# Retention attention and a GELU layer: one pipeline over six token chunks in place of two stages

## The chip, the cores and the metric

The kernel runs on one core of a Trainium2 chip. The core has five engines with a row of instructions each: TensorE (PE; PEld is its weight load), VectorE (DVE), ScalarE (ACT), GpSimd (POOL) and SyncE (SP), which here only issues transfers. ACT and POOL issue transfers too. An engine works through its row in order and waits at the head of it. SBUF is the working memory with 128 partitions; TensorE writes to PSUM, eight banks of 128 x 512 f32. The metric is device time in microseconds (us).

## The reference

Inputs are q, k and v of 4 batches, 8 heads, 768 tokens and 64 values, and two matrices. First a retention recurrence runs for each batch and head, then a dense layer with GELU over all 3072 tokens:

```python
gamma = 1.0 - 2.0 ** (-5.0 - np.arange(H))          # H = 8
scale = 1.0 / np.sqrt(D)                              # D = 64
for t in range(S):                                    # S = 768
    state = gamma * state + outer(k[:, :, t], v[:, :, t])
    y[:, :, t] = scale * (q[:, :, t] @ state)
x = y.transpose(0, 2, 1, 3).reshape(B * S, H * D)     # 3072 x 512
h = x @ w_in                                          # 512 x 2048
g = 0.5 * h * (1.0 + tanh(c * (h + 0.044715 * h**3))) # c = sqrt(2/pi)
return g @ w_out                                      # 2048 x 512, f32
```

Both kernels turn the recurrence into chunks of 128 tokens. Within a chunk, scores k.q are masked by decays and multiplied with v; what lies before the chunk enters through a 64 x 64 state of each head, which is carried on by a product of k and v.

## The kernel before, in words

It has two stages. **Attention** loops over four pairs of heads (`hp`). For a pair, POOL loads q, k and v of all batches and all six chunks (`_load_hp`, L94, L98, L102), cast from f32 to f16 on the way; every source piece is a row of 64 f32, 256 bytes. ScalarE scales q by decays (`_prep_q`, L110), VectorE scales k (`_prep_k`, L120). For each chunk, TensorE transposes q and k (L148, L153), ScalarE copies the result out of PSUM (L159), TensorE forms scores (L170), VectorE masks them (L181), and TensorE forms y within the chunk (L192), y from the state (L203) and the new state (L214). ScalarE and VectorE write y into `xT` (L222, L224), VectorE carries the state on (L228, L237).

**MoE** begins when all four pairs are done, since its first product sums over all heads. The two weight matrices are loaded by POOL in one transfer each, behind the last q, k and v (L246, L250). The loop goes over eight blocks of 384 tokens with four waves each; a wave makes four tiles h of 128 x 384 (L297, four matmuls each). GELU is written as h times a sigmoid: ScalarE copies h out of PSUM (L305), POOL squares it (L308), VectorE makes the inner polynomial in two operations (L310, L315), ScalarE takes the sigmoid (L320), VectorE multiplies (L322). The second product of the block before (L264, sixteen matmuls of 512 columns for 128 tokens) is put between the waves; VectorE copies it out (L272), SP stores it (L273).

The tile framework sets the order on each engine by its own scheduling, from the order of the code and the buffers that come free. It also gives transfers of a kind eight completion counters ("lanes") in turn: a transfer waits until the one eight before it has landed.

## Time and profile before

| | |
|---|---|
| median of the runs | 323.15 us |
| fastest run | 320.19 us |
| profiled execution, first to last instruction (its span) | 322.5 us |
| VectorE busy | 252.3 us, 78% of the span |
| TensorE busy | 241.7 us, 75% |
| TensorE's mean granted clock | 0.910 |

The profiled execution's time outside of its span isn't listed; the median of the runs lies 0.65 us above the span. A clock of 1 is 2.4 GHz, of 0.5 is 1.2 GHz. Busy matmul time counts the length of each matmul from its first read to its modelled end, and these overlap, so the pace of a row of matmuls is read from their starts. In the groups, the figures behind the bar are the busy time, the mean of one, and how long the engine stood idle just before, with the instruction whose end released it.

### The profile page before, as it was taken

The page shows a single profiled execution, that of the slowest core. Times are in us where ns is not written, and L with a number is a line of the kernel's source. Part 1 is how long each engine was busy: PE and PEld are TensorE (multiplying, and loading weights), DVE is VectorE, ACT ScalarE, POOL GpSimd, SP SyncE. Part 2 cuts the span into 40 slices and gives each one's busy share as a digit, 9 for nine tenths or more (in the row PEclk, how much of TensorE's full clock was granted, in tenths as well). Part 3 has the DMA queues.
Part 4 walks back from the last instruction along what each step waited for, and adds up shares of the span by engine and source line. Part 5 has one row for each costly group of instructions (what it writes and reads, how often), then busy time and mean ns, then how long its engine had stood idle before and what let it go on. Part 6 is the DMA issues. An engine that isn't in the chain of part 4 may idle for free.

```text
span 322.5 us, 5240 instructions
## 1 busy us (share of the span) xinstructions
PE 241.7 (75%) x1792; PEld 138.3 (43%) x1792; DVE 252.3 (78%) x528; ACT 166.6 (52%) x338; POOL 178.1 (55%) x214
## 2 busy tenths in 40 slices
PE   0257485278586786669889789869959969959985
PEld 0134373266474543325445345435524535525432
...
GB/s 138 140 138 139 141 140 136 142 142 202 196 123 0 2 0 1 2 0 33 34 35 33 35 35 33 33 34 35 34 33 29 38 33 1 67 35 0 48 84 65
DMA packets 81514, 20.82 MB, mean 65 GB/s; under 512 B 75728, under 2 KB 77776, under 8 KB 81488
## 3 DMA queue, kind: packets, MB, share of 16 engines
...
## 4 chain that ended last, share of the span: by engine, by line
DVE 64%; PE 13%; POOL 10%; issue 6%; ACT 4%; DMA 1%; DVEq 0%; ACTq 0%; POOLq 0%
DVE ww L315 23%; DVE t L310 14%; DVE g_sb L322 12%; DVE a_sb L181 8%; POOL pp L308 5%; ACT sg L320 3%; DVE kd L120 3%; PE yc_ps L203 3%; PE qkT_ps L148 3%; PE qkT_ps L153 2%; DVE s_new L228 2%; PE o_ps L264 2%; POOL qd L94 2%; POOL kp L98 2%; PE a_ps L170 1%
## 5 line engine op out<-in xcount | busy, mean ns | idle before, releaser
L308 POOL TENSOR_TENSOR pp<-hs 128x384 f16<-128x384 f16 x128 | 107.2, 858 | 129.9 <-DVE g_sb L322 64.6
L297 PE MATMUL h_ps<-xT,w_in_sb 128*128 128x384 f16 x512 | 96.1, 339 | 25.8 <-ACT hs L305 25.7
L320 ACT ACTIVATE sg<-ww 128x384 f16<-128x384 f16 x124 | 64.9, 524 | 81.7 <-DVE ww L315 81.2
L264 PE MATMUL o_ps<-w_out_sb,g_sb 128*128 128x512 f16 x384 | 87.6, 380 | 4.2 <-DVE g_sb L322 2.7
L315 DVE TENSOR_TENSOR ww<-t,hs 128x384 f16<-128x384 f16 x128 | 77.1, 602 | 7.5
L297 PEld LDWEIGHTS <-w_in_sb 128*128 128x128 f16 x512 | 51.6, 101 | 69.0 <-issue 37.6
L310 DVE TENSOR_SCALAR t<-pp 128x384 f16<-128x384 f16 x128 | 51.8, 405 | 8.7 <-POOL pp L308 8.7
L264 PEld LDWEIGHTS <-g_sb 128*128 128x128 f16 x384 | 37.5, 98 | 48.7 <-DVE g_sb L322 3.8
L305 ACT CAST hs<-h_ps 128x384 f16<-128x384 f32 x128 | 54.9, 472 | 3.3 <-PE h_ps L297 3.3
L322 DVE TENSOR_TENSOR g_sb<-hs,sg 128x384 f16<-128x384 f16 x124 | 51.1, 418 | 5.6 <-ACT sg L320 4.9
L120 DVE TENSOR_SCALAR kd<-kp,dec_sb 128x384 f16<-128x384 f16 x32 | 24.0, 774 | 20.5 <-DMA kp<-in_k_dram 20.5
L181 DVE TENSOR_TENSOR a_sb<-a_ps,msk_sb 128x512 f16<-128x512 f32 x48 | 29.2, 681 | 9.6 <-PE a_ps L170 9.6
...
L148 PE MATMUL qkT_ps<-iden_sb,qd 128*128 128x128 f16 x96 | 19.4, 294 | 17.8 <-ACT qd L110 17.4
L203 PE MATMUL yc_ps<-qkT_sb,s_new 64*64 64x128 f16 x160 | 12.7, 310 | 25.2 <-DVE s_new L228 15.7
L110 ACT ACTIVATE qd<-qd,dec_sb 128x384 f16<-128x384 f16 x32 | 19.0, 627 | 22.2 <-DMA qd<-in_q_dram 22.2
L222 ACT CAST xT<-yi_ps 128x512 f16<-128x512 f32 x24 | 13.9, 589 | 27.9 <-PE yi_ps L192 27.9
L159 ACT COPY qkT_sb<-qkT_ps 128x1024 f16<-128x1024 f16 x24 | 22.4, 1038 | 4.8 <-PE qkT_ps L153 4.8
L148 PEld LDWEIGHTS <-qd 128*128 128x128 f16 x96 | 13.1, 138 | 18.9 <-ACT qd L110 18.1
L102 POOL DMA_DIRECT2D vr<-in_v_dram x16 | 21.0, 1315 | 0.0
L224 DVE TENSOR_TENSOR xT<-xT,yc_ps 128x512 f16<-128x512 f16 x20 | 13.7, 683 | 9.2 <-PE yc_ps L203 8.2
...
## 6 DMA issues: line engine op xcount, KB each, us to landing
out_dram<-o_sb SPq DMA_DIRECT2D x24, 256.0 KB, 2.0
qd<-in_q_dram POOLq DMA_DIRECT2D x32, 96.0 KB, 4.3
kp<-in_k_dram POOLq DMA_DIRECT2D x32, 96.0 KB, 4.2
...
w_in_sb<-in_moe_w_in_dram POOLq DMA_DIRECT2D x1, 2048.0 KB, 15.5
w_out_sb<-in_moe_w_out_dram POOLq DMA_DIRECT2D x1, 2048.0 KB, 25.1
...
```

The lines of the kernel that those rows point to most:

```text
L94: nc.gpsimd.dma_start(out=qd[b][hp][:, :, j, :], in_=q[b, 2 * hp + j].rearrange("(c p) d -> p c d", p=128),)
L98: nc.gpsimd.dma_start(out=kp[b][hp][:, :, j, :], in_=k[b, 2 * hp + j].rearrange("(c p) d -> p c d", p=128),)
L148: nc.tensor.transpose(out=qkT_ps[:, b * 128:(b + 1) * 128], in_=qd[b][hp][:, c], identity=iden_sb,)
L181: nc.vector.tensor_tensor(out=a_sb[c][j], in0=a_ps[j], in1=msk_sb[:, 2 * hp + j].unsqueeze(1).broadcast_to([128, B, 128]), op=ALU.mult,)
L264: nc.tensor.matmul(out=o_ps, lhsT=g_tiles[fc][:, mi * 128:(mi + 1) * 128], rhs=w_out_sb[:, fc], start=(fc == 0), stop=(fc == 15),)
L297: nc.tensor.matmul(out=h_ps, lhsT=w_in_sb[:, kc, fc * 128:(fc + 1) * 128], rhs=xT[kc][:, bb * S + loc: bb * S + loc + MB], start=(kc == 0) ...
L305: nc.scalar.copy(out=hs[fc], in_=h_ps)
L308: nc.gpsimd.tensor_tensor(out=pp, in0=hs[fc], in1=hs[fc], op=ALU.mult)
L310: nc.vector.tensor_scalar(out=t1, in0=pp, scalar1=float(GA), scalar2=1.0, op0=ALU.mult, op1=ALU.add,)
L315: nc.vector.tensor_tensor(out=ww[fc], in0=t1, in1=hs[fc], op=ALU.mult)
L320: nc.scalar.activation(out=sg, in_=pww[fc], func=AF.Sigmoid, scale=sig_s)
L322: nc.vector.tensor_tensor(out=g_all[pmb][fc], in0=phs[fc], in1=sg, op=ALU.mult)
```

## The change

The program is one pipeline over six chunks of 128 tokens (times four batches, 512 columns for the MoE). `load` brings q, k and v of one chunk and batch as f32, 256 KB each with 1024 pieces of 256 bytes, by the queues of SP and ACT for the first chunk and SP alone later. `prep` scales q and k and casts v to f16: for the first chunk on VectorE (q), POOL (k) and ScalarE (v), later all on POOL. Attention works on one chunk and batch at a time in three pieces: T (`att_T`: eight transposes, one VectorE copy), A (`att_A`: eight score matmuls, two masks on VectorE) and Y (`att_Y`: y from the state and from the scores into one bank, the new state, VectorE's copies, and a scaling of the state on POOL). The three pieces share three PSUM banks. `moe1` makes one h tile of 512 columns and one ScalarE operation with GELU from PSUM to SBUF; `moe2` makes half of an output tile, or a share of it in the first chunk. The scheduling is switched off (`manual_schedule`), so engines keep the order of the code: `zip_units` puts the pieces of the next chunk between the matmul units of this one, twelve pieces on the first 22 of 24 units. Chunk 0 and chunk 1 split h tiles in halves of 256 columns. The weights are loaded by POOL in eight parts each. The scale of the decays moves from the mask and k to q, the mask is made on the chip from a triangle, and the state of a pair is kept as a 128 x 128 block with zeros beside its two heads.

The lines added (the lines removed are those of the listing above from the constants to the end of the function):

```diff
+    ctx.enter_context(tc.manual_schedule())
+    const = ctx.enter_context(tc.tile_pool(name="const", bufs=1))
+    ld = ctx.enter_context(tc.tile_pool(name="ld", bufs=2 * B))
+    pre = ctx.enter_context(tc.tile_pool(name="pre", bufs=2 * B))
+    att = ctx.enter_context(tc.tile_pool(name="att", bufs=3))
+    xp = ctx.enter_context(tc.tile_pool(name="xp", bufs=2))
+    gp = ctx.enter_context(tc.tile_pool(name="gp", bufs=2))
+    op = ctx.enter_context(tc.tile_pool(name="op", bufs=4))
+    psum = ctx.enter_context(tc.tile_pool(name="psum", bufs=1, space=bass.MemoryType.PSUM))
...
+    def load(c, b, engs):
+        for i, (nm, src) in enumerate(srcs):
+            t = ld.tile([128, H, Dh], F32, tag=f"{nm}32", name=f"{nm}32")
+            engs[i % len(engs)].dma_start(
+                out=t, in_=src[b, :, c * C:(c + 1) * C, :].rearrange("h p d -> p h d")
+            )
+            raw[nm, c, b] = t
+    SY, AC = nc.sync, nc.scalar
+    load(0, 0, (AC, SY, AC))
+    nc.sync.dma_start(out=iden, in_=iden_h.ap())
+    load(0, 1, (SY, AC, SY))
+    load(0, 2, (AC, SY, AC))
+    load(0, 3, (SY, AC, SY))
+    warm = const.tile([128, 1], F16)
+    nc.scalar.activation(out=warm, in_=cst[:, 0:1], func=AF.Gelu_apprx_tanh, scale=1.0)
+    st = const.tile([128, NHP, B, 128], F16, name="st")
+    nc.gpsimd.memset(st, 0.0)
...
+    for j in range(2):
+        for hp in range(NHP):
+            nc.vector.tensor_scalar(
+                out=mask[:, j, hp],
+                in0=cst[:, OT:OT + 128],
+                scalar1=float(1.0 / g128[2 * hp + j]),
+                scalar2=None,
+                op0=ALU.mult,
+            )
...
+    def prep(c, b):
+        for nm, col in (("q", OQ), ("k", OK)):
+            t = pre.tile([128, H, Dh], F16, tag=f"{nm}16", name=f"{nm}16")
+            eng = nc.vector if (c == 0 and nm == "q") else nc.gpsimd
+            eng.tensor_tensor(
+                out=t,
+                in0=raw.pop((nm, c, b)),
+                in1=cst[:, col:col + H].unsqueeze(2).broadcast_to([128, H, Dh]),
+                op=ALU.mult,
+            )
+            h16[nm, c, b] = t
+        t = pre.tile([128, H, Dh], F16, tag="v16", name="v16")
+        if c == 0:
+            nc.scalar.copy(out=t, in_=raw.pop(("v", c, b)))
+        else:
+            nc.gpsimd.tensor_copy(out=t, in_=raw.pop(("v", c, b)))
+        h16["v", c, b] = t
...
+    def att_T(c, b):
+        ps = psum.tile([128, 2, NHP, 128], F16, tag="att", bufs=3, name="qkT_ps")
+        for i, nm in ((0, "q"), (1, "k")):
+            for hp in range(NHP):
+                nc.tensor.transpose(
+                    out=ps[:, i, hp], in_=pair(h16[nm, c, b], hp), identity=iden
+                )
+        t = att.tile([128, 2, NHP, 128], F16, tag="qkT", name="qkT")
+        nc.vector.tensor_copy(out=t, in_=ps)
+        qkT[c, b] = t
...
+    def att_A(c, b):
+        t = qkT[c, b]
+        ps = [
+            psum.tile([128, NHP, 128], F32, tag="att", bufs=3, name=f"a_ps{j}")
+            for j in range(2)
+        ]
+        for hp in range(NHP):
+            for j in range(2):
+                nc.tensor.matmul(
+                    out=ps[j][:, hp],
+                    lhsT=t[j * 64:(j + 1) * 64, 1, hp],
+                    rhs=t[j * 64:(j + 1) * 64, 0, hp],
+                    start=True,
+                    stop=True,
+                )
+        for j in range(2):
+            s = att.tile([128, NHP, 128], F16, tag=f"a{j}", name=f"a_sb{j}")
+            nc.vector.tensor_tensor(out=s, in0=ps[j], in1=mask[:, j], op=ALU.mult)
+            a_sb[c, b, j] = s
...
+    def att_Y(c, b):
+        vv = h16["v", c, b]
+        kk = h16["k", c, b]
+        y_ps = psum.tile([128, NHP, 128], F32, tag="att", bufs=3, name="y_ps")
+        if c > 0:
+            for hp in range(NHP):
+                nc.tensor.matmul(
+                    out=y_ps[:, hp],
+                    lhsT=st[:, hp, b],
+                    rhs=qkT[c, b][:, 0, hp],
+                    start=(hp == 0),
+                    stop=False,
+                    skip_group_check=True,
+                )
+        for hp in range(NHP):
+            for j in range(2):
+                nc.tensor.matmul(
+                    out=y_ps[j * 64:(j + 1) * 64, hp],
+                    lhsT=vv[:, 2 * hp + j],
+                    rhs=a_sb[c, b, j][:, hp],
+                    start=(c == 0),
+                    stop=True,
+                    skip_group_check=True,
+                )
+        if c + 1 < NCk:
+            s_ps = psum.tile([128, NHP, 128], F32, tag="att", bufs=3, name="s_ps")
+            for hp in range(NHP):
+                nc.tensor.matmul(
+                    out=s_ps[:, hp], lhsT=pair(kk, hp), rhs=pair(vv, hp), start=True, stop=True
+                )
+        if b == 0:
+            xT[c] = xp.tile([128, NHP, B * C], F16, tag="x", name="xT")
+        nc.vector.tensor_copy(out=xT[c][:, :, b * C:(b + 1) * C], in_=y_ps)
+        if c + 1 < NCk:
+            for j in range(2):
+                sl = slice(j * 64, (j + 1) * 64)
+                if c == 0:
+                    nc.vector.tensor_copy(out=st[sl, :, b, sl], in_=s_ps[sl, :, sl])
+                else:
+                    nc.vector.tensor_tensor(
+                        out=st[sl, :, b, sl],
+                        in0=s_ps[sl, :, sl],
+                        in1=stg[sl, :, b, sl],
+                        op=ALU.add,
+                    )
+            if c + 2 < NCk:
+                nc.gpsimd.tensor_tensor(
+                    out=stg[:, :, b],
+                    in0=st[:, :, b],
+                    in1=cst[:, OG:OG + NHP].unsqueeze(2).broadcast_to([128, NHP, 128]),
+                    op=ALU.mult,
+                )
...
+    NQ = 8
...
+    w_in_sb = [const.tile([128, NHP, FQ * 128], F16, name=f"w_in{i}") for i in range(NQ)]
+    w_out_sb = [const.tile([128, FQ, d_model], F16, name=f"w_out{i}") for i in range(NQ)]
...
+    def load_w_in(i):
+        nc.gpsimd.dma_start(
+            out=w_in_sb[i],
+            in_=moe_w_in.rearrange("(kc p) n -> p kc n", p=128)[
+                :, :, i * FQ * 128:(i + 1) * FQ * 128
+            ],
+        )
...
+    def moe1(c, fc, t0=0, t1=B * C):
+        h_ps = psum.tile([128, B * C], F32, tag="h", bufs=3, name="h_ps")
+        for kc in range(NHP):
+            nc.tensor.matmul(
+                out=h_ps[:, t0:t1],
+                lhsT=w_in_sb[fc // FQ][:, kc, (fc % FQ) * 128:(fc % FQ + 1) * 128],
+                rhs=xT[c][:, kc, t0:t1],
+                start=(kc == 0),
+                stop=(kc == NHP - 1),
+            )
+        if t0 == 0:
+            g_sb[c, fc] = gp.tile([128, B * C], F16, tag=f"g{fc}", name="g")
+        nc.scalar.activation(
+            out=g_sb[c, fc][:, t0:t1],
+            in_=h_ps[:, t0:t1],
+            func=AF.Gelu_apprx_tanh,
+            scale=1.0,
+        )
+    o_ps = {}
...
+    def moe2(c, b, fcs, tag="o", bufs=2):
+        if fcs[0] == 0:
+            o_ps[c, b] = psum.tile([128, d_model], F32, tag=tag, bufs=bufs, name="o_ps")
+        ps = o_ps[c, b]
+        for fc in fcs:
+            nc.tensor.matmul(
+                out=ps,
+                lhsT=g_sb[c, fc][:, b * C:(b + 1) * C],
+                rhs=w_out_sb[fc // FQ][:, fc % FQ],
+                start=(fc == 0),
+                stop=(fc == NF - 1),
+            )
+        if fcs[-1] == NF - 1:
+            o_sb = op.tile([128, d_model], F32, tag="o", name="o_sb")
+            if b == B - 1:
+                nc.vector.tensor_copy(out=o_sb, in_=ps)
+            else:
+                nc.scalar.copy(out=o_sb, in_=ps)
+            nc.sync.dma_start(out=out[b * S + c * C:b * S + (c + 1) * C, :], in_=o_sb)
...
+    def zip_units(units, pieces):
+        done = 0
+        for i, u in enumerate(units):
+            u()
+            want = min(len(pieces), ((i + 1) * len(pieces) + len(units) - 1) // len(units))
+            while done < want:
+                fn[pieces[done][0]](pieces[done][1], int(pieces[done][2]))
+                done += 1
+    for b in range(B):
+        prep(0, b)
+        if b == 2:
+            for i in range(NQ):
+                load_w_in(i)
+    for i in range(NQ):
+        load_w_out(i)
+    for b in range(B):
+        load(1, b, (SY,))
+    run(0, "T0 T1 A0 T2 A1 Y0 T3 A2 Y1 A3 Y2")
+    half = 2 * C
+    for fc in range(0, 2):
+        moe1(0, fc, 0, half)
+    run(0, "Y3")
+    for fc in range(2, 8):
+        moe1(0, fc, 0, half)
+    for fc in range(0, 8):
+        moe1(0, fc, half, 2 * half)
+    for fc in range(8, 16):
+        moe1(0, fc)
+    for b in range(B):
+        prep(1, b)
+    for b in range(B):
+        load(2, b, (SY,))
+    units = [
+        (lambda e=e: [
+            moe2(0, b, [2 * e, 2 * e + 1], *(("o", 2) if b < 2 else ("h", 3)))
+            for b in range(B)
+        ])
+        for e in range(8)
+    ]
+    zip_units(units, [(p[0], 1, p[1]) for p in "T0 T1 A0 A1 Y0 Y1".split()])
+    def std_pieces(c):
+        return [
+            (p[0], c, p[1]) for p in "T0 T1 A0 T2 A1 Y0 T3 A2 Y1 A3 Y2 Y3".split()
+        ]
+    for c in range(1, NCk):
+        if c + 2 < NCk:
+            for b in range(B):
+                load(c + 2, b, (SY,))
+        if c == 1:
+            units = [(lambda fc=fc: moe1(c, fc, 0, half)) for fc in range(NF)]
+            zip_units(units, [(p[0], 1, p[1]) for p in "T2 T3 A2 A3 Y2 Y3".split()])
+            units = [(lambda fc=fc: moe1(c, fc, half, 2 * half)) for fc in range(NF)]
+        else:
+            units = [(lambda fc=fc: moe1(c, fc)) for fc in range(NF)]
+        units += [
+            (lambda b=b, hf=hf: moe2(c, b, list(range(hf * 8, hf * 8 + 8))))
+            for b in range(B)
+            for hf in range(2)
+        ]
+        pieces = []
+        if c + 1 < NCk:
+            for b in range(B):
+                prep(c + 1, b)
+            pieces = std_pieces(c + 1)
+        if pieces:
+            zip_units(units[:-2], pieces)
+            for u in units[-2:]:
+                u()
+        else:
+            for u in units:
+                u()
```

ScalarE in the MoE. Before, in the middle of the stage (`hs` is the copy of h, `sg` the sigmoid):

```order
L320 ACTIVATE sg<-ww 128x384
L305 CAST hs<-h_ps 128x384 x2
L320 ACTIVATE sg<-ww 128x384 x4
L305 CAST hs<-h_ps 128x384 x3
L320 ACTIVATE sg<-ww 128x384
```

Now, from the last cast of v for the first chunk to the output copies of chunk 1 (`g` is the GELU's result):

```order
L119 CAST v_169<-v_107 128x512
L249 ACTIVATE g<-h_ps 128x256 x16
L249 ACTIVATE g<-h_ps 128x512 x8
L275 COPY o_sb<-o_ps 128x512 x3
L249 ACTIVATE g<-h_ps 128x256 x32
L275 COPY o_sb<-o_ps 128x512 x3
```

The copies and sigmoids that alternate on ScalarE have become one operation a tile; output copies stand between the chunks.

VectorE at the start of the program. Before (`kd` is the scaled k):

```order
L120 TENSOR_SCALAR kd_0_0_87<-kp_0_86,dec_sb 128x384 x2
L120 TENSOR_SCALAR kd_1_0_96<-kp_0_95,dec_sb 128x384 x2
L120 TENSOR_SCALAR kd_2_0_105<-kp_0_104,dec_sb 128x384 x2
L120 TENSOR_SCALAR kd_3_0_114<-kp_0_113,dec_sb 128x384 x2
L120 TENSOR_SCALAR kd_0_1_139<-kp_1_138,dec_sb 128x384
L181 TENSOR_TENSOR a_sb_257<-a_ps_247,msk_sb 128x512
L181 TENSOR_TENSOR a_sb_259<-a_ps_248,msk_sb 128x512
```

Now (`q` are the four scaled q of chunk 0, `qkT` the transposed q and k, `a_sb` masked scores, `st` the state):

```order
L96 TENSOR_SCALAR mask<-cst 128x128 x8
L110 TENSOR_TENSOR q_139<-q_84,cst 128x512
L110 TENSOR_TENSOR q_145<-q_91,cst 128x512
L110 TENSOR_TENSOR q_151<-q_97,cst 128x512
L110 TENSOR_TENSOR q_165<-q_103,cst 128x512
L139 COPY qkT<-qkT_ps 128x1024 x2
L159 TENSOR_TENSOR a_sb_235<-a_ps_225,mask 128x512
L159 TENSOR_TENSOR a_sb_237<-a_ps_226,mask 128x512
L139 COPY qkT<-qkT_ps 128x1024
L159 TENSOR_TENSOR a_sb_260<-a_ps_250,mask 128x512
L159 TENSOR_TENSOR a_sb_262<-a_ps_251,mask 128x512
L195 CAST xT<-y_ps 128x4x128
```

All four scalings of q stand ahead of the first copy of transposed q and k, which ScalarE made before.

POOL behind the loads of the weights. Before:

```order
L102 DMA vr_3_901<-in_v_dram 128x12x64
L246 DMA w_in_sb<-in_moe_w_in_dram 128x4x2048
L250 DMA w_out_sb<-in_moe_w_out_dram 128x16x512
L308 ISA
L308 TENSOR_TENSOR pp<-hs 128x384 x128
```

Now (`stg` is the state scaled for the next chunk, `q`, `k` and `v` are those of chunk 1):

```order
L230 DMA w_out_137<-in_moe_w_out_dram 128x2x512
L230 DMA w_out_138<-in_moe_w_out_dram 128x2x512
L209 TENSOR_TENSOR stg<-st,cst 128x4x128 x4
L110 TENSOR_TENSOR q_536<-q_179,cst 128x512
L110 TENSOR_TENSOR k_538<-k_181,cst 128x512
L121 CAST v_540<-v_183 128x512
L110 TENSOR_TENSOR q_542<-q_185,cst 128x512
```

The squares are gone; scalings of the state and then those of the next chunk's q and k stand behind the last weight transfer, and in each later chunk again four `stg` ahead of the next `q`.

## Rows read from the trace of the kernel before

**Rows 1.** The page, part 1: busy us, share of the span, instructions.
```profile
PE 241.7 (75%) x1792; PEld 138.3 (43%) x1792; DVE 252.3 (78%) x528; ACT 166.6 (52%) x338; POOL 178.1 (55%) x214
```

**Rows 2.** Windows of three stretches: length, busy us of each engine, granted clock, DMA.
```profile
core 0: us, PE busy (x) PEld busy (x) DVE busy (x) ACT busy (x) POOL busy (x), PEclk, DMA share, GB/s
20.00:111.50 91.50, 61.63 (x872) 46.94 (x872) 69.06 (x112) 49.06 (x73) 51.98 (x61) 0.76 1.51 127
111.50:309.50 198.00, 168.91 (x863) 85.69 (x861) 175.97 (x401) 110.57 (x255) 107.22 (x128) 0.97 0.07 27
309.50:322.50 13.00, 8.07 (x35) 3.34 (x35) 3.85 (x9) 0.98 (x2) 0.00 (x0) 1.00 0.21 81
```

**Rows 3.** The page, part 4: the chain of waits by line.
```profile
DVE ww L315 23%; DVE t L310 14%; DVE g_sb L322 12%; DVE a_sb L181 8%; POOL pp L308 5%; ACT sg L320 3%; DVE kd L120 3%; PE yc_ps L203 3%; PE qkT_ps L148 3%; PE qkT_ps L153 2%; DVE s_new L228 2%; PE o_ps L264 2%; POOL qd L94 2%; POOL kp L98 2
```

**Rows 4.** The page, part 5: groups of the MoE stage (columns: heading of part 5).
```profile
## 5 line engine op out<-in xcount | busy, mean ns | idle before, releaser
L297 PE MATMUL h_ps<-xT,w_in_sb 128*128 128x384 f16 x512 | 96.1, 339 | 25.8 <-ACT hs L305 25.7
...
L264 PE MATMUL o_ps<-w_out_sb,g_sb 128*128 128x512 f16 x384 | 87.6, 380 | 4.2 <-DVE g_sb L322 2.7
L315 DVE TENSOR_TENSOR ww<-t,hs 128x384 f16<-128x384 f16 x128 | 77.1, 602 | 7.5
...
L310 DVE TENSOR_SCALAR t<-pp 128x384 f16<-128x384 f16 x128 | 51.8, 405 | 8.7 <-POOL pp L308 8.7
L322 DVE TENSOR_TENSOR g_sb<-hs,sg 128x384 f16<-128x384 f16 x124 | 51.1, 418 | 5.6 <-ACT sg L320 4.9
```

**Rows 5.** Timeline of TensorE (start us, length us): attention, first slow, later fast.
```profile
20.46 0.29 PE L148 MATMUL qkT_ps<-iden_sb,qd 128*128 128x128 f16 x1 [3.52 <-ACT qd L110]
...
21.18 0.31 PE L153 MATMUL qkT_ps<-iden_sb,kp 128*128 128x128 f16 x1
...
46.89 0.22 PE L153 MATMUL qkT_ps<-iden_sb,kp 128*128 128x128 f16 x1
...
47.79 0.22 PE L153 MATMUL qkT_ps<-iden_sb,kp 128*128 128x128 f16 x1
47.94 0.62 PE L170 MATMUL a_ps<-qkT_sb 64*128 64x128 f16 x16
...
51.22 0.41 PE L192 MATMUL yi_ps<-a_sb,vr 128*64 128x128 f16 x7
```

**Rows 6.** DMA packets from 10 to 60 us, and issues (KB each, us to landing).
```profile
DMA packets 54666, 6.95 MB, mean 139 GB/s; under 512 B 54661, under 2 KB 54661, under 8 KB 54661
...
out_dram<-o_sb SPq DMA_DIRECT2D x24, 256.0 KB, 2.0
qd<-in_q_dram POOLq DMA_DIRECT2D x32, 96.0 KB, 4.3
...
w_out_sb<-in_moe_w_out_dram POOLq DMA_DIRECT2D x1, 2048.0 KB, 25.1
```

**Rows 7.** Single lines: operation, count: duration ns min/median/max, first and last start, shape.
```profile
L181 DVE TENSOR_TENSOR a_sb<-a_ps,msk_sb x48: 677/680/693, 24.6 to 102.3; 128x512 f16<-128x512 f32 x48
...
L222 ACT CAST xT<-yi_ps x24: 564/586/640, 29.0 to 110.5; 128x512 f16<-128x512 f32 x24
...
L237 DVE CAST s_new<-st_ps x4: 410/410/414, 32.4 to 102.9; 128x256 f16<-128x256 f32 x4
...
L159 ACT COPY qkT_sb<-qkT_ps x24: 1012/1034/1072, 20.9 to 96.4; 128x1024 f16<-128x1024 f16 x24
...
L272 DVE COPY o_sb<-o_ps x24: 677/684/692, 147.6 to 318.6; 128x512 f32<-128x512 f32 x24
...
L315 DVE TENSOR_TENSOR ww<-t,hs x128: 344/360/999, 114.8 to 309.8; 128x384 f16<-128x384 f16 x128
...
L308 POOL TENSOR_TENSOR pp<-hs x128: 820/827/1033, 113.6 to 308.3; 128x384 f16<-128x384 f16 x128
```

**Rows 8.** Timeline of the end, all engines (start us, length us).
```profile
311.24 7.30 PE L264 MATMUL o_ps<-w_out_sb,g_sb 128*128 128x512 f16 x33 [0.35 <-DVE g_sb L338]
311.81 7.82 SPq L273 DMA_DIRECT2D out_dram<-o_sb  x4
```

303 lines of the change are left out of this document (33 added, 270 removed).

## The prediction

> **What bounds the kernel now.** I read the page first, for busy times, then the stages by windows, then the chain of waits, then the groups of the long stage, and last the pace of single matmuls. VectorE is busiest at 252.3 us, TensorE has 241.7 [rows 1]. In the table by stage the reader is to see three stretches: up to 111.5 us attention runs while the loads come in, with TensorE at a mean clock of 0.76; from there to 309.5 us the MoE runs with VectorE busy 176.0 of 198.0 us; 13 us end it [rows 2]. The chain runs over VectorE lines L315, L310 and L322, the GELU written out [rows 3]. Their groups sum to 77.1 + 51.8 + 51.1 = 180 us [rows 4], the MoE stage itself. The same stage's matmuls need less: 33 of 512 columns take 7.30 us, so (7.30 - 0.38)/32 = 0.216 us each, at full clock [rows 8]; all MoE work is 768 such matmuls (512 of 384 columns are worth 384, and 384 of 512 [rows 4]), or **166 us**. So half of the span lies in two places: 111 us before the first MoE matmul, and 32 us of the stage in which TensorE waits for VectorE.
>
> **What goes.** The GELU chain (POOL square, three VectorE operations, a ScalarE copy and a sigmoid per tile) leaves; one ScalarE operation from PSUM stands for it. A ScalarE cast of 128x512 out of PSUM takes 0.586 us [rows 7]; no row shows GELU, but the sigmoid is one table function per tile too and is no multiple of a copy, so I take 0.59 (0.37 for half a tile). 72 whole and 48 half tiles are 60 us in all; each stands behind 4 matmuls of 0.216, so 0.59 runs under 0.86. I cost it at nothing; its cover is gone only above 0.86 us a tile. VectorE loses 180 us and keeps evacuations: per (chunk, batch) a qkT copy, two masked scores at 0.68, y at about 0.68, two state pieces at about 0.41 [rows 7], some 4.4 us, 24 times, or about 105 us of the run. VectorE bounds nothing after the opening. **TensorE does.**
>
> **TensorE's work.** MoE 166 us. Attention per (chunk, batch): 8 transposes and 8 full matmuls (4 from the state, 4 for it) of 128 columns at (47.79 - 46.89)/16 = 0.056 us; 8 score and 8 y matmuls that run in pairs, 0.62 us for 16 and 0.41 for 7, so about 0.03 each [rows 5]. That is 0.9 + 0.5 = 1.4 us; the first chunk has no state to read and the last none to write. 20 pairs after the first chunk give 27 us less 20 x 0.05 for the last chunk, 26 us. Remaining after the opening: 166 + 26 = **192 us**.
>
> **The opening.** Twelve loads of 1024 pieces of 256 bytes, spread over the queues of SP and ACT, replace the loads from POOL that cast. Before, 54661 such pieces passed in 50 us, 0.915 ns each, so 0.94 us for a load if the new queues are as quick; if they didn't overlap at all a load would cost the 4.3 us that one of 768 pieces takes to land; a store of 256 KB lands in 2.0 [rows 6]. I take 0.94, since its pieces are the same reads of 256 bytes, and keep the other end for the rivals. VectorE has all four q scalings in its row before the first qkT copy, so it waits for the fourth q, which is about the tenth load: 1 + 10 x 0.94 + 2 to land + 0.75 to scale = 13 us. From there VectorE's own row sets the time: 3 copies before y of batch 0, one after, 3 masked pairs, y and state of batch 0, y of batch 1. For a copy of 1024 f16 from PSUM no row of VectorE exists; 512 f32 take 0.684, so 1.22 us by element, and ScalarE took 1.034 for it [rows 7]. With 1.22: 4 x 1.22 + 3 x 1.36 + 1.5 + 0.7 = 11 us, then y's state pieces and the fourth pair's first half, which free the two score banks, 1.5 us, and about 1.5 for handing on at three banks, with transposes at the 0.103 us of the first ones [rows 5]. The first MoE matmul starts at **27 us** (20 to 37). The Trainium skill (VectorE: DVE Perf Modes, The perf-mode tier table) has a copy of 16-bit data from PSUM at up to twice the rate. By that the four copies would cost 2.2 us less and the sum 2 us less; no run here shows it.
>
> The weights come beside. Before, both were issued together and had landed after 25.1 us [rows 6], at most 1.6 us for each of the sixteen pieces. POOL issues the first at about 11 us, and the second chunk's loads (11 us of transfer) share the rings, so the last piece of w_in lands between 11 + 13 + 2 = 26 and 37 us; it is asked for at 27 + 12. No wait, or one of 1 us. POOL is held by its row: the last w_out issue waits for a lane that the last w_in frees, then four state scalings, then the second chunk's q and k. POOL's two-input operation takes 0.827 us for 384 elements [rows 7], so 1.1 for 512. From 37 us: 4.4 + 2.2 more is 44; TensorE asks at 27 + 14 + 1.7 = 43. I take 0 to 1 us here, inside the small waits below.
>
> **Stalls at the seams.** In POOL's row the scaling of a chunk stands behind the last state scaling of the chunk before it, and that behind VectorE's state pieces of the last batch. From the end of that piece on TensorE: 1.7 us VectorE, 1.1 state, 2.2 for q and k, so 5 to 6 us; each further batch 2.9 (a cast of v at about 0.6). In the chunks with whole tiles TensorE has 3 pieces of 1.73 and one of 0.86 us to do first, 6 us; the first batch doesn't wait, the second about 1 us. Three chunks, 3 us. In chunk 1 the units are half tiles of 0.43 us, and the last piece lies three units before: TensorE waits about 4, then 2, then 0.5 us, **6 us**, and in this stage idle stretches of 2 us have gone with a clock under 1 (0.97 on the mean [rows 2]); I add 2 us. Sixty pieces in chunks 1 to 5 wait a little for a bank or a copy; before, TensorE waited 4.2 us in all ahead of 384 o matmuls, always for VectorE [rows 4], so I put 0.08 us on each, 5 us (0 to 18).
>
> **The end** is as before: from the last matmul (311.24 + 7.30) to the end of the span 4 us, with copy and store [rows 8].
>
> **Sum:** 27 + 192 + 3 + 6 + 2 + 5 + 4 = 239 us of span, against 322.5. The median of the runs lies 0.65 us over that span, so **240 us**.
>
> **The rivals.**
> (a) *The forecast*, 228 to 254: TensorE bound from about 27 us, with seams of 1 to 6 us. 0.62.
> (b) *No seams.* If POOL's operations are shorter or VectorE copies in half the time, the opening ends near 22 and waits shrink to 4 us: 22 + 192 + 4 + 4 = 222, up to 228. For it: POOL's row above is for 384 f16 elements and VectorE's for f32. Against it: the order in POOL's row is fixed. 0.13.
> (c) *Slower loads.* Pieces of 256 bytes on the queues of SP and ACT have no row. At 2 us a load the fourth q comes 10 us later: 250. At 3 us, 20 later, and twelve loads take 36 us while a chunk has 33 us of TensorE work (27.6 MoE and 5.4 attention): 262. For it: the store's 2.0 and the landing of 4.3 us. Against it: those are times of one, and many are in flight. 0.14, over 250 to 290.
> (d) *VectorE's evacuations held by POOL.* L315 reads two SBUF operands and took 0.344 to 0.999 us, with POOL's square beside it; the copy out of PSUM, L272, stayed within 0.677 to 0.692 [rows 7]. The masked scores and state sums read PSUM and one SBUF operand, and no row shows one beside POOL arithmetic. If each is held half of the time for 0.6 us, forty pieces slip by 0.5 us: 260. The Trainium skill (GPSIMD Engine Reference, Key points) says that POOL shares its SBUF interfaces with VectorE and that two SBUF inputs collide; L315 agrees, and by that page these operations, with one, would not. 0.08.
> (e) *Slower than before: loads set the pace of all.* Seventy-two loads at x us, and after the last of them about 45 us (scaling, the last attention, its MoE of 28 us, the end): 72x + 45. It passes 323 at x = 3.9 us and 329 at 3.95, so it decides where loads hardly overlap, at the landing time of 4.3 us. Against it: before, pieces of the same size passed at 0.94 us per 1024 with several landing at once. 0.03.
>
> The likeliest time is 240. To hold 8 in 10 the range takes (a) whole, most of (b) and the nearer half of (c) and (d): **222 to 264**. A change under 2% can't be told from none here. Faster by more: (a) to (d), 0.96; the same: a strip of (e), 0.01; slower: 0.03.
>
> **What will show it.** First qkT copy on VectorE near 13 us and first h matmul near 27. Twelve loads landed by 16 us. GELU at about 0.59 us and under 0.86. In chunks 2 to 4 a period of 34 to 36 us, with TensorE idle before transposes, released by POOL's q or k. In chunk 1 three such waits, the first of about 4 us. The matmul pace of 0.216 unchanged. If TensorE's idle time lies before score or y matmuls, released by VectorE, (d) is right; if before transposes, with POOL waiting for loads, (c) or (e). The forecast is wrong if TensorE is idle for more than 25 us after the first h matmul.

## The result: 239.1 us, and the profile after

The changed kernel takes 239.13 us (median of 4 runs, 238.1 to 240.66), the kernel before 323.94 in the runs beside it: a ratio of 0.7413, 95% interval 0.735 to 0.7477. The ratio leaves out one of the four runs of the kernel before, a slow one of 477 us, which the median of 323.94 includes. The forecast was 240. The profiled execution took 239.32 us, with a span of 237.5 us and a mean granted clock of 0.986.

The page of the changed kernel, part 1 (busy us, share of the span, instructions), part 4 (the chain of waits) and part 5 (groups, columns as in [rows 4]):

```profile
PE 216.5 (91%) x1600; PEld 118.6 (50%) x1600; DVE 87.0 (37%) x154; ACT 75.5 (32%) x144; POOL 85.8 (36%) x101
...
PE 85%; POOL 5%; DMA 5%; DVE 2%; SPq 1%; issue 1%; POOLq 0%
...
L240 PE MATMUL h_ps<-xT,w_in 128*128 128x512 f16 (+1 forms) x480 | 93.8, 344 | 0.0
L263 PE MATMUL o_ps<-w_out,g 128*128 128x512 f16 x384 | 86.9, 379 | 0.0
L249 ACT ACTIVATE g<-h_ps 128x512 f16<-128x512 f32 (+1 forms) x120 | 61.4, 512 | 76.1 <-PE h_ps L240 74.7
```

Against [rows 1] VectorE falls from 252.3 to 87.0 us, and TensorE, busy for 75% of a longer span, is busy for 91% of this one. The chain, which ran over three VectorE lines [rows 3], is TensorE's own work for 85%. Ahead of the h and o matmuls it stood idle for 25.8 and 4.2 us [rows 4]; now 0.0 for both. ScalarE, with GELU, waits 74.7 us for h_ps, and no wait of TensorE ends on ScalarE.

The same kernel's windows (columns as in [rows 2]), cut at the first h matmul and around chunk 1's seam, and five microseconds inside that seam:

```profile
0.00:24.50 24.50, 10.76 (x100) 7.22 (x101) 13.95 (x30) 3.75 (x6) 14.37 (x20) 1.00 1.18 219
24.50:60.00 35.50, 35.50 (x270) 21.50 (x268) 11.43 (x22) 13.63 (x30) 20.09 (x23) 1.00 1.17 209
60.00:80.00 20.00, 16.73 (x169) 12.30 (x169) 9.51 (x16) 7.75 (x21) 12.28 (x14) 0.83 1.02 251
80.00:220.00 140.00, 140.00 (x1011) 71.68 (x1006) 51.44 (x87) 48.30 (x85) 39.07 (x45) 1.00 0.29 78
...
72.00:77.00 5.00, 4.51 (x32) 2.86 (x30) 1.38 (x2) 0.99 (x3) 5.00 (x7) 0.50 0.95 214
```

The 111.5 us ahead of the first MoE matmul [rows 2] are 24.5. From there TensorE is idle in one place only, between 60 and 80 us (3.3 us), and that is also the only one of the four windows with a granted clock under 1: 0.83 on the mean, and 0.50, the level of 1.2 GHz, from 72 to 77 us. The last 64 matmuls start at 219.54 us, so the end is 4 us behind them, as in [rows 8]:

```profile
219.54 13.98 PE L263 MATMUL o_ps<-w_out,g 128*128 128x512 f16 x64
```

TensorE's longest waits behind its start are one of 4.1 us for VectorE's first qkT copy, in the opening, and one of 2.2 us for a q that POOL scales. Its timeline at the second place (start us, length us; idle before and releaser in brackets):

```profile
70.86 0.45 PE L135 MATMUL qkT_ps<-iden,q 128*128 128x128 f16 x4 [2.22 <-POOL q L110]
71.86 0.61 PE L135 MATMUL qkT_ps<-iden,k 128*128 128x128 f16 x4 [0.56 <-POOL k L110]
...
74.42 0.61 PE L135 MATMUL qkT_ps<-iden,k 128*128 128x128 f16 x4 [0.39 <-POOL k L110]
74.82 1.91 PE L240 MATMUL h_ps<-xT,w_in 128*128 128x256 f16 x8
...
78.41 0.39 PE L135 MATMUL qkT_ps<-iden,q 128*128 128x128 f16 x4
...
78.86 1.04 PE L240 MATMUL h_ps<-xT,w_in 128*128 128x256 f16 x8
```

The seam of chunk 1 (the place where chunk 2's first pieces wait for POOL) has three waits for POOL's scalings, 2.22, 0.56 and 0.39 us. After the first of them four transposes take 0.61 us and eight matmuls of 256 columns 1.91; at 78.4 the same take 0.39 and 1.04. So the seam costs twice: the idle time, and about as much again in slow matmuls.

Where the forecast's terms went (forecast, then measured, us):

| term | forecast | after |
|---|---|---|
| first h matmul | 27 | 24.55 |
| MoE, 768 matmuls of 0.216 | 166 | 166: 64 in 13.98, or 0.216 each |
| attention of 20 pairs | 26 (1.4 each, less 1 in all) | 34.7 (1.78 each, less 0.9) |
| seams of chunks 2 to 4 | 3 | 0 |
| seam of chunk 1, idle and clock | 6 + 2 | 3.3 + 3.1 |
| small waits | 5 | about 0 |
| end | 4 | 4.0 |
| not assigned by the forecast | | 1.9 |
| span | 239 | 237.5 |

Of the 1.9 us, 0.7 are chunk 0's last piece (26.39 to 27.10 us) and 1.0 are the first eight matmuls of 256 columns at the slow pace (1.84 us from start to the next start, for 0.87 at 0.109 each); 0.2 is unassigned. The 3.1 is counted from the timeline: from 70.86 to 78.41 us lie 0.95 us of idle time and matmuls that take 3.5 at the full pace. An experiment below gives the same.

### The profile page after: what moved, and what is told of

Read it like the earlier page. It is cut to its first block, busy times and chain, and to the rows that moved or that the text cites. A ratio compares the mean times of both kernels' runs of the same rounds, so it can differ in the third digit from the quotient of the medians.

```text
span 237.5 us, 3948 instructions
## 1 busy us (share of the span) xinstructions
PE 216.5 (91%) x1600; PEld 118.6 (50%) x1600; DVE 87.0 (37%) x154; ACT 75.5 (32%) x144; POOL 85.8 (36%) x101
## 4 chain that ended last, share of the span: by engine, by line
PE 85%; POOL 5%; DMA 5%; DVE 2%; SPq 1%; issue 1%; POOLq 0%
PE h_ps L240 35%; PE o_ps L263 35%; PE qkT_ps L135 4%; PE y_ps L179 3%; DMA k<-in_k_dram 3%; PE a_ps L150 3%; POOL w_in L222 3%; PE s_ps L190 2%; PE y_ps L169 2%; POOL k L110 2%; DMA v<-in_v_dram 2%; SPq L72 1%; DVE a_sb L159 1%; POOL q L110 0%; DVE st L202 0%
## 5 line engine op out<-in xcount | busy, mean ns | idle before, releaser
L240 PE MATMUL h_ps<-xT,w_in 128*128 128x512 f16 (+1 forms) x480 | 93.8, 344 | 0.0
L263 PE MATMUL o_ps<-w_out,g 128*128 128x512 f16 x384 | 86.9, 379 | 0.0
L249 ACT ACTIVATE g<-h_ps 128x512 f16<-128x512 f32 (+1 forms) x120 | 61.4, 512 | 76.1 <-PE h_ps L240 74.7
L240 PEld LDWEIGHTS <-w_in 128*128 128x128 f16 x480 | 45.7, 100 | 32.0 <-issue 0.2
L263 PEld LDWEIGHTS <-g 128*128 128x128 f16 x384 | 36.5, 98 | 41.6
L159 DVE TENSOR_TENSOR a_sb<-a_ps,mask 128x512 f16<-128x512 f32 x48 | 30.9, 686 | 24.6 <-PE a_ps L150 24.3
L209 POOL TENSOR_TENSOR stg<-st,cst 128x512 f32<-128x512 f16 x16 | 16.5, 1040 | 49.3 <-DVE st L202 48.0
L195 DVE CAST xT<-y_ps 128x512 f16<-128x512 f32 x24 | 16.6, 691 | 35.0 <-PE y_ps L179 35.0
L110 POOL TENSOR_TENSOR k<-k,cst 128x512 f16<-128x512 f32 x24 | 25.1, 1046 | 7.0 <-DMA k<-in_k_dram 7.0
L110 POOL TENSOR_TENSOR q<-q,cst 128x512 f16<-128x512 f32 x20 | 20.9, 1043 | 2.8 <-DMA q<-in_q_dram 2.8
```

The lines of the kernel that those rows point to most:

```text
L110: eng.tensor_tensor(out=t, in0=raw.pop((nm, c, b)), in1=cst[:, col:col + H].unsqueeze(2).broadcast_to([128, H, Dh]), op=ALU.mult,)
L159: nc.vector.tensor_tensor(out=s, in0=ps[j], in1=mask[:, j], op=ALU.mult)
L195: nc.vector.tensor_copy(out=xT[c][:, :, b * C:(b + 1) * C], in_=y_ps)
L209: nc.gpsimd.tensor_tensor(out=stg[:, :, b], in0=st[:, :, b], in1=cst[:, OG:OG + NHP].unsqueeze(2).broadcast_to([128, NHP, 128]), op=ALU.mult,)
L240: nc.tensor.matmul(out=h_ps[:, t0:t1], lhsT=w_in_sb[fc // FQ][:, kc, (fc % FQ) * 128:(fc % FQ + 1) * 128], rhs=xT[c][:, kc, t0:t1], start= ...
L249: nc.scalar.activation(out=g_sb[c, fc][:, t0:t1], in_=h_ps[:, t0:t1], func=AF.Gelu_apprx_tanh, scale=1.0,)
```

## The experiments

The theory: TensorE sets the end; the gain is VectorE's 180 us taken off GELU, which lets attention lie between MoE matmuls under the loads; what is left to win is the seam of chunk 1 and the opening. The rivals that were tried: one half of the change does it all; the loads set the pace; the opening is bound by something other than its order.

**The changed kernel again**, as the base of the runs on the same chip.

> The changed kernel as it is, timed on the same chip as the three variants sent with it: 237 to 241 us, ratio 0.735 to 0.748.

239.19 us, ratio 0.7447 [0.7409, 0.7485], span 236.9. The opening differs a little between executions: here the first h matmul starts at 23.73 us and the first o matmul at 39.43, in the execution above at 24.55 and 40.12.

**GELU alone**: the kernel before, with one ScalarE operation for the six.

```diff
-            nc.scalar.copy(out=hs[fc], in_=h_ps)
...
-            nc.vector.tensor_tensor(out=ww[fc], in0=t1, in1=hs[fc], op=ALU.mult)
+            nc.scalar.activation(out=g_all[mb][fc], in_=h_ps,
+                                 func=AF.Gelu_apprx_tanh, scale=1.0)
```

> The kernel before with GELU as one ScalarE operation and nothing else changed. If the MoE stage then runs at TensorE's pace: 111.5 us before it, 166 to 174 in it, 5 at the end, so 283 to 291 us, ratio 0.88 to 0.90. If GELU made most of the gain: 260 or less. If it made nothing of it: 315 or more.

285.26 us, ratio 0.8819 [0.8746, 0.8893]. The window of its MoE stage:

```profile
111.50:270.00 158.50, 158.50 (x854) 83.98 (x853) 15.21 (x22) 62.72 (x128) 0.00 (x0) 0.99 0.09 34
```

TensorE is never idle in it; the stage ahead, with 61.6 us of 91.5 busy, is that of [rows 2]. 38 us of the 84 are GELU's, and 46 are left to the rest of the change.

**The pipeline with GELU written out** as before (ScalarE copy and POOL square at once; `gelu2`, two VectorE operations, two tiles later; `gelu3`, the sigmoid and VectorE's product, another two later; ahead of the second half of each output tile, and of every unit of `moe2` in chunk 0, all pending tiles are finished at once).

```diff
-        nc.scalar.activation(
-            out=g_sb[c, fc][:, t0:t1],
...
+        nc.scalar.copy(out=hs[:, :n], in_=h_ps[:, t0:t1])
+        nc.gpsimd.tensor_tensor(out=pp[:, :n], in0=hs[:, :n], in1=hs[:, :n], op=ALU.mult)
+        stage.append([g_sb[c, fc][:, t0:t1], hs, pp, None, n])
+        if len(stage) >= 3:
+            gelu2(stage[-3])
+            if len(stage) >= 5:
+                gelu3(stage.pop(0))
```

> The pipeline and its loads, but GELU written out as in the kernel before (copy on ScalarE, square on POOL, two operations on VectorE, sigmoid on ScalarE, product on VectorE), each step one or two tiles behind. If TensorE bounds only because VectorE lost 180 us: VectorE has 87 + 180 = 267 us, and the run takes 275 to 300 us. If the pipeline alone makes the gain: 245 or less. If GELU alone made it: 315 or more.

383.66 us, ratio 1.1886 [1.1792, 1.1981]: far slower than the first two theories allowed. It lies in the open range of the third (315 or more), but not for its reason, since GELU alone brought only 38 us. And with more buffers for the copy of h, its square and the product (10 for 6, 4 for 3, 6 for 4; one fewer, 2 for 3, between VectorE's two operations) and the last step two columns further back, six behind its h in place of four:

> The pipeline with GELU written out, as in the run of 383.7 us, with more buffers (10 instead of 6 for the copy of h, 4 instead of 3 for its square, 6 instead of 4 for the product) and the last step four columns later than before. Rival A (the order and the buffers held it): 300 to 335 us, the waits of ScalarE for VectorE's g fall to a third. Rival B (VectorE and POOL themselves: each column takes VectorE's three and POOL's one operation, which together with the attention's keep VectorE's row longer than TensorE's): 355 us or more, VectorE busy over 70% still.

389.77 us, ratio 1.2114 [1.2026, 1.2202], with VectorE busy for 72%, as its rival B had it: these buffers were not it. The first one's page (parts 1 and 4) and its waits:

```profile
PE 263.2 (69%) x1600; PEld 132.3 (35%) x1600; DVE 271.1 (71%) x514; ACT 127.0 (33%) x264; POOL 203.4 (53%) x221
...
DVE 55%; PE 14%; POOL 12%; issue 11%; DMA 6%; SPq 1%; ACT 1%; POOLq 0%; DVEq 0%; ACTq 0%
```

```profile
ACT hs L253 <- DVE g L277: 77.6, 48, 4.2
...
DVE o_sb L305 <- PE o_ps L295: 30.1, 6, 13.3
PE h_ps L242 <- ACT hs L253: 28.5, 18, 11.1
DVE xT L196 <- PE y_ps L180: 28.0, 10, 5.0
```

VectorE has the chain (55%) but is idle for 111 us: it waits 58 us for TensorE's o and y, and TensorE waits for ScalarE's copy of h, and that for VectorE's g. With the order written out, GELU's VectorE steps and attention's stand in one row, and each waits behind the other. In this written order the pipeline is no gain by itself: alone it loses 61 us, with GELU on ScalarE it brings 46. How much of the 111 us another written order would recover, one without the points at which all pending tiles are finished above all, was not tried, so rival B's reason (VectorE's own work) is not shown.

**Attention first**, the rest as changed: all pieces of a chunk in a row, chunk by chunk, then the MoE; all six chunks' xT kept.

```diff
+    for c in range(NCk):
...
+        run(c, "T0 T1 A0 T2 A1 Y0 T3 A2 Y1 A3 Y2 Y3")
+    for c in range(NCk):
+        for fc in range(NF):
+            moe1(c, fc)
+        for b in range(B):
+            moe2(c, b, list(range(NF)))
```

> The changed kernel with the attention of all six chunks first and the MoE after it; loads, GELU and operations are the same. If the pipeline's worth is to hide loads and the attention's waits: 72 loads at 0.94 us and the weights beside them end near 85 to 95 us, the MoE of 166 us and the end of 4 follow: 255 to 268 us. If only TensorE's work counts and waits are few: 240.

301.52 us, ratio 0.9364 [0.9295, 0.9433]: a miss of over 33 us. Its windows up to the first h matmul and from there, POOL's timeline around chunk 3's scalings (the last state scaling of chunk 2, the last k of chunk 3, the last state scaling of chunk 3), and the transfers from 45 to 80 us:

```profile
0.00:129.50 129.50, 72.29 (x737) 48.78 (x737) 80.12 (x147) 3.75 (x6) 85.60 (x101) 0.86 0.90 180
129.50:295.00 165.50, 165.50 (x770) 75.06 (x768) 4.28 (x7) 67.84 (x114) 0.00 (x0) 1.00 0.10 37
```

```profile
80.23 1.04 POOL L209 TENSOR_TENSOR stg<-st,cst 128x512 f32<-128x512 f16 x1 [0.62 <-DVE st L202]
...
89.89 1.04 POOL L110 TENSOR_TENSOR k<-k,cst 128x512 f16<-128x512 f32 x1
...
100.43 1.04 POOL L209 TENSOR_TENSOR stg<-st,cst 128x512 f32<-128x512 f16 x1 [0.62 <-DVE st L202]
```

```profile
DMA packets 32698, 8.30 MB, mean 237 GB/s; under 512 B 32685, under 2 KB 32694, under 8 KB 32694
```

The loads cost a little more than forecast: 35 us / 32,698 packets is 1.07 ns each, 1.1 us for a load of 1024, against 0.94, with almost nothing else beside them. But they do not set the pace. From 60 us on a chunk takes 20.2 us (60.03, 80.23 and 100.43 for the last state scaling), and its twelve loads only 13. It is a round of waits: POOL scales the next chunk's q, k and v (10 us), TensorE and VectorE work through its last batch, POOL scales its last state, and only then come the next chunk's scalings. That is chunk 1's seam in every chunk, without a MoE to fill it; no scaling waits for a load after 49.85 us. TensorE waits for POOL's q 31.8 us in all, 12.9 of them at chunk 1, whose scalings stand behind the w_out issues. The granted clock is 0.86 on the mean. Weaving attention into the MoE is worth 62 us against this order; with the scalings ahead of the last state scalings, as tried below for chunk 2, it would be worth less, and how much was not tried. The MoE itself takes 165.5 us, as in the forecast.

**Every load twice**, the second into a spare tile.

```diff
+            d = ld.tile([128, H, Dh], F32, tag="spare", bufs=8, name="spare")
+            engs[i % len(engs)].dma_start(
+                out=d, in_=src[b, :, c * C:(c + 1) * C, :].rearrange("h p d -> p h d")
```

> The changed kernel with every load of q, k and v issued twice, the second into a spare tile that nothing reads; the 288 loads are spread over the same queues. Theory (TensorE sets the pace, loads matter in the opening only): the loads of chunk 0 are doubled, some 10 us more before the first h matmul, which comes at 24.6 in the changed kernel; from chunk 1 on a chunk needs 24 loads of about 1.1 us (the continuous loads of the kernel with attention first), 26 us of a chunk's 34.75, so they stay hidden: 247 to 254 us. Rival (loads set the pace as soon as there are more of them, because a load costs more beside the running engines): 4 chunks of 40 us or more instead of 34.75, waits of PE for POOL q and k in every chunk, 265 to 285 us.

258.36 us, ratio 0.8022 [0.7972, 0.8073]: between the two. TensorE's longest waits behind the first h matmul, and a later window:

```profile
50.36 0.40 PE L139 MATMUL qkT_ps<-iden,k 128*128 128x128 f16 x4 [2.25 <-POOL k L114]
...
58.41 0.61 PE L139 MATMUL qkT_ps<-iden,q 128*128 128x128 f16 x4 [5.92 <-POOL q L114]
...
90.14 0.45 PE L139 MATMUL qkT_ps<-iden,q 128*128 128x128 f16 x4 [2.23 <-POOL q L114]
```

```profile
120.00:150.00 30.00, 30.00 (x224) 15.26 (x223) 12.94 (x22) 10.72 (x18) 12.62 (x15) 1.00 1.05 249
```

The first h matmul comes at 30.6 us, 6 later. Chunk 1's pieces then wait 2.25, 5.92 and 1.87 us for q and k that POOL scales late because their loads land late; up to about 53 us the weights still land beside them. The wait at 90.14 is the seam of chunk 1, which the changed kernel has at 70.86 too: it comes 19.3 us later here, and the whole run is 19.2 us longer. So all of the loss lies ahead of it: 6 us of opening, 10 of waits, and 3 that are left for the lower clock behind these waits. From there on nothing is lost, although the transfers go on at 249 GB/s. The changed kernel's own loads are hidden (12 x 1.1 = 13 us of a chunk's 34.75), and from chunk 2 on twice as many are (26 us). The theory held there and missed chunk 1, whose loads share the transfers with the weights.

**The weights first**: POOL issues w_in and w_out ahead of its first scaling.

```diff
-        prep(0, b)
-        if b == 2:
+        if b == 0:
             for i in range(NQ):
                 load_w_in(i)
-    for i in range(NQ):
-        load_w_out(i)
+            for i in range(NQ):
+                load_w_out(i)
+        prep(0, b)
```

> The changed kernel with both weight matrices issued by POOL ahead of its first scaling, so that they share the rings with the loads of the first chunk. If the opening is set by those loads, the first qkT copy comes 8 to 14 us later and the run takes 247 to 253 us. If it is set by VectorE's and POOL's rows, there is no change, 239.

255.93 us, ratio 0.7937 [0.7885, 0.7989], 17 more than the changed kernel and more than either theory had. VectorE's timeline, its fourth scaling of q and its first copy, and POOL's, the last of its w_out issues and its scalings of k:

```profile
24.39 0.69 DVE L110 TENSOR_TENSOR q<-q,cst 128x512 f16<-128x512 f32 x1 [8.45 <-DMA q<-in_q_dram]
30.51 0.69 DVE L139 COPY qkT<-qkT_ps 128x1024 f16<-128x1024 f16 x1 [5.43 <-PE qkT_ps L135]
```

```profile
27.95 0.71 POOL L230 DMA_DIRECT2D w_out<-in_moe_w_out_dram  x1 [1.34 <-DMA w_in<-in_moe_w_in_dram]
28.75 4.04 POOL L110 TENSOR_TENSOR k<-k,cst 128x512 f16<-128x512 f32 x4
```

The first qkT copy comes at 30.51 us in place of 13.63, and two things add up to these 16.9 us. The fourth q lands 11.4 us later beside the weights (its scaling starts at 24.39 in place of 13.02), which is the first theory's 8 to 14. And each w_out issue waits for a lane, and so for a part of w_in to land; POOL's scalings of k stand behind eight of these waits, and hold the copy for another 5.4 us. So an issue costs what it holds up in its row, besides what it moves.

**Chunk 2's scaling early**: POOL scales chunk 2's q, k and v ahead of the last state scalings of chunk 1.

```diff
+            for b in range(B):
+                prep(2, b)
             units = [(lambda fc=fc: moe1(c, fc, 0, half)) for fc in range(NF)]
...
-            for b in range(B):
+            for b in range(B if c > 1 else 0):
                 prep(c + 1, b)
```

> Chunk 2's q, k and v are scaled by POOL before the last two state scalings of chunk 1, so T of chunk 2 finds them ready. If the seam costs what its waits and the half clock behind them show (3.2 us of waits and about 3 us of slow matmuls), the run is 5 to 6 us shorter than the changed kernel, 233 to 234 us, and the granted clock stays at 1 from 60 to 80 us. If the waits alone count, 3 us. If the wait only moves to the next piece (state scalings late for Y of chunk 2), no change.

232.8 us, ratio 0.7242 [0.7209, 0.7275], clear of the changed kernel's interval. The window of the seam:

```profile
60.00:80.00 20.00, 20.00 (x252) 16.47 (x251) 14.86 (x26) 10.72 (x28) 11.71 (x14) 1.00 1.01 250
```

Idle time and low clock are both gone. The medians differ by 6.4 us. The spans (231.1 against 236.9 of the run beside it) differ by 5.8, but include openings that differ by 0.7 (first o matmul at 40.15 here). Between the first o matmul and the last 64 lie 173.0 us here:

```profile
40.15 1.89 PE L263 MATMUL o_ps<-w_out,g 128*128 128x512 f16 x8
...
213.15 13.98 PE L263 MATMUL o_ps<-w_out,g 128*128 128x512 f16 x64
```

In the run beside it they are 179.5 us (39.43 to 218.96), and 179.4 in the execution above. Of these 6.5 us 3.3 were idle time, so about 3.2 were matmuls at the lower clock, as the expectation had it.

**The opening in another order** (each batch's scaling directly ahead of its pieces, so that VectorE's first copy does not stand behind all four q scalings), alone and with the edit above.

```diff
+    prep(0, 0)
+    run(0, "T0")
+    prep(0, 1)
+    run(0, "T1 A0")
...
+    run(0, "T2 A1 Y0 A2 Y1")
+    prep(0, 3)
...
+    run(0, "T3 Y2")
```

> In the opening the scalings stand just ahead of their pieces, and the pieces that need batch 3 come after those that don't. If VectorE's row (four q scalings ahead of the first copy) sets the first h matmul, it comes at about 21 us in place of 24.6, and with 1 us given back to a late third part of w_in the run is 2 to 3 us shorter, 236 to 237. If the loads or the first part of w_in set it (landed before 19.3 us), it comes at 24 or later and the time does not change.

> Both edits. If opening and seam are separate terms of one sum, the gains add: 7 to 9 us shorter than the changed kernel, 230 to 232. If what is gained in the opening is waited for in the seam (POOL is bound to the loads of chunk 1), only the larger of the two remains, about 234.

240.2 us, ratio 0.748 [0.7441, 0.7519], and 233.6 us, 0.7265 [0.7233, 0.7297], beside the 239.19 and 232.8 of the same kernels without it: no gain. TensorE's timeline of the first:

```profile
20.25 0.61 PE L135 MATMUL qkT_ps<-iden,q 128*128 128x128 f16 x4 [2.10 <-DVE q L110]
22.15 0.61 PE L135 MATMUL qkT_ps<-iden,k 128*128 128x128 f16 x4 [1.29 <-POOL k L110]
...
23.66 1.91 PE L240 MATMUL h_ps<-xT,w_in 128*128 128x256 f16 x8
```

The first h comes at 23.66 us, no earlier than the 23.73 of the run beside it. The first pieces do come earlier, but batch 3's q and k are scaled late, behind VectorE's y and state work and behind POOL's first state scalings, and TensorE waits 2.10 and 1.29 us for them. The first o matmul starts at 40.19 us, against 39.43 and 40.12 in the two executions of the changed kernel: work changed places, idle time did not go.

**An early first h**: batch 3's scaling directly behind the w_in issues, and the pieces of batches 2 and 3 between the first h columns, on top of chunk 2's early scaling. Then the same with w_out in four parts, so that POOL's row holds four waiting issues.

```diff
-    run(0, "T0 T1 A0 T2 A1 Y0 T3 A2 Y1 A3 Y2")
+    run(0, "T2 A1 Y0 A2 Y1")
     half = 2 * C
     for fc in range(0, 2):
         moe1(0, fc, 0, half)
+    run(0, "T3 Y2")
+    for fc in range(2, 4):
+        moe1(0, fc, 0, half)
+    run(0, "A3")
...
-    w_out_sb = [const.tile([128, FQ, d_model], F16, name=f"w_out{i}") for i in range(NQ)]
+    w_out_sb = [const.tile([128, 4, d_model], F16, name=f"w_out{i}") for i in range(4)]
```

> The kernel with chunk 2's scaling moved ahead (232.8 us), and an opening in which the scaling of batch 3 stands in POOL's row directly behind the four w_in issues, and the pieces of chunk 0's later batches stand between the first columns of the MoE. Theory: the first h matmul comes at 19 to 20 us instead of 24.6, and TensorE is idle 1 to 2.5 us less in all: 230.5 to 232.8 us. Rival (the earlier reordering of the opening gained nothing because POOL's row, with the w_out issues waiting for w_in's parts until about 34 us, sets when chunk 1's q and k are scaled, whatever the order before it): 232.5 to 234 us, with the first h earlier and a wait of PE for POOL at 35 to 42 us in its place.

> The kernel of the run beside this one (early h), with w_out loaded in four parts instead of eight, so that POOL's row holds four issues that wait for a part of w_in to land instead of eight. Theory (POOL's row is what held the opening's gain): POOL reaches the state scalings and chunk 1's q at about 26 us instead of 35, and the gain of the earlier first h is kept: 229 to 231 us. Rival (the opening is bound by TensorE's own work and the landing of w_out, which does not come earlier): same as the run beside this one within 0.5 us.

230.94 us, ratio 0.7173 [0.7128, 0.7217], and 230.2 us, 0.7152 [0.7108, 0.7195]. The timelines of TensorE, of the first and then of the second:

```profile
18.99 1.86 PE L240 MATMUL h_ps<-xT,w_in 128*128 128x256 f16 x8 [0.61 <-DVE xT L195]
...
37.01 1.89 PE L263 MATMUL o_ps<-w_out,g 128*128 128x512 f16 x8
39.06 0.40 PE L135 MATMUL qkT_ps<-iden,q 128*128 128x128 f16 x4 [0.16 <-POOL q L110]
40.06 0.40 PE L135 MATMUL qkT_ps<-iden,k 128*128 128x128 f16 x4 [0.60 <-POOL k L110]
```

```profile
39.23 0.39 PE L135 MATMUL qkT_ps<-iden,q 128*128 128x128 f16 x4
```

The first h comes at 19 us; the o matmuls start 2.4 to 3.1 us earlier than in the two executions of the changed kernel, and POOL's scalings of chunk 1 then come 1 us late (0.16, 0.60 and a later 0.22). With four parts POOL begins the state scalings at 24.3 us in place of 34.0, that wait is gone, and 230.2 us is the fastest version here. The two intervals overlap, so that the four parts bring 0.7 us is read from the waits and the times (229.98 to 230.62 us against 230.55 to 231.28), not from the ratios. Together the edits take 8.9 us off the changed kernel's median.

## Why the prediction was right

**What bounds**: right. VectorE's three GELU lines went, TensorE sets the end, and GELU alone gave 38 us where the forecast counted 32. It had set all 166 us of MoE work against the 198 of a stretch that ends ahead of the last 33 matmuls [rows 8]; up to the end of these (318.54 us) it is 207, and the difference 41.

**GELU** takes 0.597 us per whole tile and 0.384 per half, taken as 0.59 and 0.37, under its cover of 0.86.

**The opening**: first qkT copy at 13.6 us (13), first h at 24.55 (27). The failed part is the price of the copy from PSUM, taken as 1.22 us by element from a f32 row [rows 7]. Single lines of the changed kernel (duration ns min/median/max, first and last start):

```profile
L139 DVE COPY qkT<-qkT_ps x24: 681/692/693, 13.6 to 185.8; 128x1024 f16<-128x1024 f16 x24
L195 DVE CAST xT<-y_ps x24: 681/692/693, 18.1 to 200.6; 128x512 f16<-128x512 f32 x24
```

1024 f16 take as long as 512 f32. Four copies at 0.53 less are 2.1 of the 2.5 us. The Trainium skill (VectorE: DVE Perf Modes, The perf-mode tier table) has a copy of 16-bit data from PSUM at up to twice the rate; the measured 0.692 agrees, and the forecast's own estimate by that rule, 2 us less, would have been 25.

**TensorE's work**: the MoE's 0.216 held; a pair of chunk and batch was 0.38 us too cheap. Three pieces of chunk 1 on the timeline, one each of T, A and Y:

```profile
41.84 0.39 PE L135 MATMUL qkT_ps<-iden,q 128*128 128x128 f16 x4
...
42.29 1.89 PE L263 MATMUL o_ps<-w_out,g 128*128 128x512 f16 x8
...
46.62 3.63 PE L263 MATMUL o_ps<-w_out,g 128*128 128x512 f16 x16
50.18 0.40 PE L150 MATMUL a_ps<-qkT 64*128 64x128 f16 x8
50.51 1.90 PE L263 MATMUL o_ps<-w_out,g 128*128 128x512 f16 x8
52.24 0.39 PE L169 MATMUL y_ps<-qkT,st 128*128 128x128 f16 x4
52.56 0.41 PE L179 MATMUL y_ps<-a_sb,v 128*64 128x128 f16 x8
52.91 0.40 PE L190 MATMUL s_ps<-v,k 128*128 128x128 f16 x4
53.14 1.89 PE L263 MATMUL o_ps<-w_out,g 128*128 128x512 f16 x8
```

From start to start T takes 0.45 us (8 x 0.056, as forecast); A takes 0.33 where 0.24 was counted, and about 0.1 more goes ahead of it (16 matmuls of 0.216 are 3.45, and it starts 3.56 behind them); Y takes 0.90 in steps of 0.32, 0.35 and 0.23, where 0.22, 0.24 and 0.22 were counted. So about 0.1 us is lost four times in a pair: into A and out of it, and into the second step of Y and out of it. These are the changes between matmuls on 128 x 128 of the array and those on half of it (`64*128` and `128*64` in the rows); between transposes and MoE matmuls nothing is lost. The forecast had priced long runs of one form, and [rows 5] already has one such change: the score matmuls start 0.15 us behind the last transpose (47.79 to 47.94), where the transposes stand 0.056 apart. Twenty pairs: 8 us.

**The waits**: the 5 us of small waits did not come (no wait over 0.3 us outside of seam and opening), nor the 3 us in chunks 2 to 4. There the first h matmuls of chunks 2 to 5 start at 102.38, 137.13, 171.88 and 205.73 us, periods of 34.75, 34.75 and 33.85 (the last chunk's attention writes no state). They fit the forecast's 34 to 36 by two errors that cancel: 27.6 of MoE work with 7.1 of attention and no idle time, in place of 5.4 and 1. The seam's chain was counted too long. From the end of the last state matmuls (97.37 us) to the second batch's k VectorE and POOL need 7.0 us (ready at 104.40), where the forecast had 5 to 6 and 2.9 more; TensorE's own work up to the transposes that read it (104.78) is 7.4. Chunk 1's seam was forecast at 8 with the clock and cost 6.4; its first wait, for q and k together, was 2.8, not 4.

**From the span to the time**: the forecast added 0.65 us, the difference of a span and a median of other executions. The profiled execution itself took 1.8 us more than its span (239.32 and 237.5).

So the errors cancel: attention +8.7 and what was not assigned +1.9 on one side; opening -2.5, small waits -5, seams -4.6 on the other. They leave 1.5 us of span. The mechanism was right, the precision of one microsecond was luck.

**The rivals.** (b), no seams: nearly so, and the opening was 24.55 and not 22; the dearer attention pieces kept the time from 222. (c) and (e): the loads run at 1.1 us when they never pause, far from the 2 to 4 us that these rivals need. (d): POOL's work does not hold these evacuations; a masked score takes 0.679 to 0.693 us, 0.677 to 0.693 before [rows 7]. In the run with GELU written out VectorE's product g of two SBUF operands, beside POOL's squares, took 0.833 us on the mean for a whole tile and up to 1.264, and its masked score out of PSUM, of as many elements, 0.673 to 0.692. The Trainium skill's rule on two SBUF inputs (GPSIMD Engine Reference, Key points), which the forecast cited, agrees with both.
